# Five of sixteen weight pieces get their low halves from TensorE sums; VectorE scales four early pairs; 24 unread matmuls go; the main decay moves to the seventh step

## The chip, the cores and the metric

The kernel runs on one core of one Trainium2 chip. Time is device microseconds for one execution of the program; the smaller the better. The engines are TensorE (PE, with PEld for its weight loads), VectorE (DVE), ScalarE (ACT), GpSimd (POOL) and SyncE (SP), whose queue issues the DMAs.

## The reference

Attention with a forget gate over 8 batches of 8 heads (576 tokens, head size 64), and a two-layer feed-forward network with a leaky ReLU on its 4608 x 512 result:

```python
def _attn_ref(q, k, v, f):
    scores = scale * np.matmul(q, k.transpose(0, 1, 3, 2))
    log_f = np.log(np.clip(f, 0.0001, 1.0))
    cum = np.cumsum(log_f, axis=-1)
    decay = cum[:, :, :, None] - cum[:, :, None, :]
    scores = np.where(causal, -1000000000.0, scores + decay)
    scores = scores - np.max(scores, axis=-1, keepdims=True)
    attn = np.exp(scores)
    attn = attn / (np.sum(attn, axis=-1, keepdims=True) + 1e-09)
    return np.matmul(attn, v)
def _moe_ref(x, w_in, w_out):          # 512 -> 2048 -> 512
    h = x @ w_in
    g = np.maximum(0.01 * h, h)
    return g @ w_out
```

q, k, v and f arrive in fp32, and the two weight matrices in fp64.

## The kernel before

Products that need fp32 accuracy are made from fp32r matmuls of split operands: a value is a high part (`..h`, the value rounded to fp32r) and a low part (`..l`, the rest), and three products (high x high, low x high, high x low) are summed in PSUM.

**Weights.** The matrices are cut into 16 *pieces* of 128 x 1024 (numbered from 0; even ones of `w_in`, odd ones of `w_out`). `fetch_weight` brings a piece's 1 MB of raw 64-bit numbers into one of two buffers `wraw`, `load_weight` makes `wh` and `wl` of it: ACT scales the upper words to fp32 (`wt`, L177) and copies them to `wh` (L185); DVE shifts `wt` (L180), then builds the low part from the mantissa bits of both words (L186 to L191). `wt` has one buffer, so the next piece's L177 waits until the last reader of `wt` is through. A `wraw` buffer is free for piece n + 2 when L191 of piece n is done.

**Early steps.** Before the main loop come twelve steps `x` = 0 to 11 (the first to the twelfth), one for each pair of heads of the first three batches, over their first 256 tokens. `early_scores` makes fp32 scores on PE (`sce`), adds the decay by a second matmul (`both`), takes the maxima on DVE (L303, `ze`, `maxe`) and the exponentials on ACT (L307), and scales the rows by the inverse sums (L315, on ACT). `early_values` transposes (`tre`), copies to `pte` on ACT (L327), multiplies by v (`ave`) and splits the result to `xh`, `xl`. In the first six steps `warm` adds matmuls of zeros that nobody reads, after each of the two parts of the scores. Each step also loads one or two more weight pieces (`WQ`), and from the fifth on it fills in quanta of the feed-forward network (`FQ`): `h` (first layer), `g`, `gh`, `gl` (activation, split), `o` (second layer, PSUM tags `o0` and `o1` with one buffer each). `decay_rows` makes the decay rows of the main loop from the running sum `fc`, and writes them to DRAM (`dec_k`, `dec_q`) for the main heads.

**Main loop.** Then 64 heads pass over PE in turn, with feed-forward quanta between their parts.

**What sets the order.** The code is written in the order of the steps; a scheduler sets the order of instructions on each engine and in SP's queue when the program is built. Each engine then works strictly in that order, and waits on semaphores. SP too: a DMA whose buffer is not free holds up those behind it.

Of the kernel before, what the change touches and what calls it, by code (L numbers as in the profile page):

```python
# [8 lines left out]
F32 = mybir.dt.float32  # L9
F32R = mybir.dt.float32r  # L10
I32 = mybir.dt.int32
U32 = mybir.dt.uint32
AF = mybir.ActivationFunctionType
ALU = mybir.AluOpType

P = 128
# [12 lines left out]
FQ = (0, 0, 0, 0, 4, 8, 8, 8, 8, 8, 8, 4, 2)  # L29
BUFS = dict(s1=2, m1=2, ost=2)  # L30
RAWS = ("ph", "pl")
WARM = (20, 4, 6)
NEG = -1.0e30
REBIAS = 2.0**-112
SIGN = -(2.0**32)
# [3 lines left out]
def forgetting_attention_ffn(ctx, tc, qT, kT, v4, vr, f, w_in, w_out, out):  # L39
# [6 lines left out]
    nc = tc.nc  # L46
# [4 lines left out]
    HPB = NHEAD // NB  # L51
# [18 lines left out]
    def width(i):  # L70
        return min((i + 1) * P, S)
# [23 lines left out]
    one = ctx.enter_context(tc.tile_pool(name="one", bufs=1))  # L95
    dram = ctx.enter_context(tc.tile_pool(name="dram", bufs=1, space=bass.MemoryType.DRAM))
    psum = ctx.enter_context(tc.tile_pool(name="psum", bufs=2, space=bass.MemoryType.PSUM))
# [9 lines left out]
    def matmul(*args, **kw):  # L107
        work[0] += 1
        nc.tensor.matmul(*args, **kw)  # L109
# [7 lines left out]
    def warm(n):  # L117

        ps = psum.tile([P, 512], F32, tag="h", name=f"warm_{len(warmed)}")
        warmed.append(n)  # L120
        for _ in range(n):
            matmul(ps, still[:, :P], still, start=True, stop=True)

    warm(WARM[0])
    eye = one.tile([P, P], F32, tag="part0", name="eye")
    make_identity(nc, eye)
    ident_r = one.tile([P, P], F32R, name="ident_r")
    nc.vector.tensor_copy(ident_r, eye)
    ident = ident_r.bitcast(F32)
    both = one.tile([P, P + T + NHEAD], F32R, tag="s1", name="both", bufs=2)  # L130
    pick = both[:, P + T:]
    nc.vector.tensor_tensor(pick, ident[:, :NHEAD], ident[:, NHEAD:], op=ALU.add)
# [27 lines left out]
    def fetch_weight(n):  # L160
        raw = raws[n] = one.tile([P, 2, 4 * P, 2], I32, tag=RAWS[n % 2], name=f"wraw_{n}")
        for k, src in enumerate(wpieces[n][0]):
            nc.sync.dma_start(raw[:, k].rearrange("p w two -> p (w two)"), src)

    def load_weight(n):


        loaded.append(n)
        _, wh, wl = wpieces[n]
        wh, wl = (w.rearrange("p c f -> p (c f)") for w in (wh, wl))  # L170
        if n not in raws:
            fetch_weight(n)
        raw = raws[n].rearrange("p m w two -> p (m w) two")
        lo, hi = raw[:, :, 0], raw[:, :, 1]
        t = one.tile([P, 8 * P], I32, tag="vs", name=f"wt_{n}")
        tf = t.bitcast(F32)
        first = nc.scalar.activation(tf, hi.bitcast(F32), AF.Prelu, scale=REBIAS, alpha=SIGN)  # L177
        if n == 0:
            tc.keep_in_program_order(first)
        first = nc.vector.tensor_scalar(  # L180
            t, t, 3, 4, op0=ALU.logical_shift_left, op1=ALU.bitwise_or
        )
        if n == 0:
            tc.keep_in_program_order(first)
        nc.scalar.copy(wh, tf)  # L185
        nc.vector.tensor_scalar(hi, hi, 23, None, op0=ALU.logical_shift_left)  # L186
        nc.vector.scalar_tensor_tensor(
            lo, lo, 9, hi, op0=ALU.logical_shift_right, op1=ALU.bitwise_or
        )
        nc.vector.tensor_scalar(hi, t, -0x800000, None, op0=ALU.bitwise_and)  # L190
        nc.vector.scalar_tensor_tensor(  # L191
            wl, lo, 2.0**-43, hi.bitcast(F32), op0=ALU.mult, op1=ALU.mult
        )

    def weights(n):
        while len(loaded) < min(n, len(wpieces)):
            load_weight(len(loaded))
# [17 lines left out]
    for i, r in enumerate(decay_r):  # L215
        n = width(i)
# [6 lines left out]
    def decay_rows():  # L223

        tc.keep_in_program_order(
            nc.vector.tensor_scalar(fc, fc, -1.0 / SCALE, None, op0=ALU.mult)
        )
        start = one.tile([P, S], F32, tag="x", name="start")
        for i in range(NCH):
            c = slice(i * P, width(i))  # L230
            nc.vector.tensor_scalar(
                start[:, c], fc[:, c], 0.0, fc[:, i * P:i * P + 1], op0=ALU.mult, op1=ALU.subtract
            )
        for name, tag, x, to in (("fck", "s1", fc, dec_k), ("fcq", "m1", start, dec_q)):
            r = one.tile([P, S], F32R, tag=tag, name=name, bufs=2)
            halves(r, x)
            for w in range(2):
                nc.sync.dma_start(to[:, w], r[w * NHEAD:(w + 1) * NHEAD].bitcast(F32))
# [4 lines left out]
    def load(t):  # L243

        s, c0, c1 = tasks[t]
        h = state[t] = {}
        a, n = c0 * P, S
        x = h["raw"] = one.tile([P, S], F32, tag="qraw", name=f"raw_{t}")
        for y, src in ((x[:D, a:n], qT[s][:, a:n]), (x[D:, :n], kT[s][:, :n])):
            last = nc.sync.dma_start(y, src)  # L250
            if t < 2:
                tc.keep_in_program_order(last)
        if s % 2 == 0:
            pairs[s // 2, c0] = {}

    def load_v(t):

        g, o = tasks[t][0] // 2, tasks[t][0] % 2
        vm = fixed["vm"]
        for y, src in ((vm[:, :NFULL], v4[g][:, o]), (vm[:REST, NFULL], vr[g][:, o])):  # L260
            last = nc.sync.dma_start(y, src)
            if t < 1:
                tc.keep_in_program_order(last)
# [3 lines left out]
    def early_load(b, g):  # L267

        e = early[b, g] = {}
        x = e["qk"] = one.tile([P, 2, T], F32, tag="b2", name=f"qk_{b}_{g}", bufs=B2)  # L270
        for y, src in enumerate((qT, kT)):
            nc.sync.dma_start(
                x[:, y], src[b * HPB + 2 * g:b * HPB + 2 * g + 2, :, :T].rearrange("s d n -> (s d) n")
            )
        v = e["v"] = one.tile([P, 2, T // P, D], F32, tag="b2", name=f"ve_{b}_{g}", bufs=B2)
        nc.sync.dma_start(v, v4[b * HPB // 2 + g][:, :, :T // P])

    def early_scores(b, g):
        e = early[b, g]
        mx = one.tile([P, 4], F32, tag="max", name=f"maxe_{b}_{g}", bufs=3)  # L280
        sm = one.tile([P, 4], F32, tag="sum", name=f"sume_{b}_{g}", bufs=3)
        for i in range(2):
            n = width(i)
            ps = [
                psum.tile([P, 512], F32, tag="sc", name=f"sce_{b}_{g}_{2 * o + i}")[:, :n]
                for o in range(2)
            ]
            for o in range(2):
                x = e["qk"][o * D:(o + 1) * D]
                matmul(ps[o], x[:, 0, i * P:n], x[:, 1, :n], start=True, stop=False)  # L290
            for o in range(2):
                s = b * HPB + 2 * g + o
                matmul(
                    ps[o], pick[:, s:s + 1].broadcast_to([P, P]), decay_r[i],
                    start=False, stop=True,
                )
            for o in range(2):
                c = 2 * o + i
                tag = ZE[g % 2][c]
                z = e[c] = one.tile(  # L300
                    [P, n], F32, tag=tag, name=f"ze_{b}_{g}_{c}", bufs=BUFS.get(tag, 1)
                )
                nc.vector.tensor_tensor_reduce(  # L303
                    out=z, in0=ps[o], in1=tri[:, TRI - n:], scale=-SCALE, scalar=3.0e38,
                    op0=ALU.add, op1=ALU.min, accum_out=mx[:, c:c + 1],
                )
                nc.scalar.activation(  # L307
                    z, z, AF.Exp, bias=mx[:, c:c + 1], scale=-1.0, accum_out=sm[:, c:c + 1]
                )
            if b * HPB // 2 + g < WARM[2]:  # L310
                warm(WARM[1])
        nc.vector.tensor_scalar(sm, sm, 1.0e-9, None, op0=ALU.add)
        nc.vector.reciprocal(sm, sm)
        for c in range(4):
            nc.scalar.activation(e[c], e[c], AF.Copy, scale=sm[:, c:c + 1])  # L315

    def early_values(b, g):
        e = early[b, g]
# [390 lines left out]
    for x, (b, g) in enumerate(steps + [(NE, 0)]):  # L709
        if x + 1 < len(steps):  # L710
            early_load(*steps[x + 1])
        if x < len(steps):
            early_scores(b, g)
            if x in (8, 11):
                load(x // 11)
            if x == 8:
                load_v(0)
            if x == 10:
                split(0)
            weights(sum(WQ[:x + 1]))  # L720
        if x == 2:
            decay_rows()
        if x:
            early_values(*steps[x - 1])
            if steps[x - 1][1] == HPB // 2 - 1:
                ready[0] = (steps[x - 1][0] + 1) * T
        if x == len(steps):
            split(1)
        fill(FQ[x])
# [73 lines left out]
```

## Time and profile before

| | us |
|---|---|
| median of 3 runs (lowest, highest) | 1214.53 (1214.12, 1217.29) |
| the profiled execution | 1215.27 |
| its span, first to last instruction | 1213.2 |
| TensorE busy | 1197.9 (99%) |
| VectorE, ScalarE, GpSimd busy | 619.5, 637.1, 460.5 |
| `warm` matmuls | 68, between 1.5 and 59.5 us |

TensorE is busy nearly all the time, and the chain of work that ended last is 94% TensorE. A busy share does not say that the matmuls are needed, nor that they run at full clock: the column of the granted clock (1.00 is full) and the names have to be read with it. A row of a timeline gives the start, the duration of the merged run, the engine, the line, what is written from what is read, the shape and the count; what stands in brackets is the idle time before it and what ended it. A row of a group gives the count, the busy time in us and the mean of one in ns, then the idle time before.

### The profile page before, as it was taken

The numbers are of one execution on the slowest core, as the hardware profiler recorded it, in microseconds if no ns is written. First come the engines' busy times: TensorE is split into PE (matmuls) and PEld (weight loads), VectorE is DVE, ScalarE is ACT, GpSimd is POOL, SyncE is SP. The second block draws the span as 40 slices with busy tenths as digits, with TensorE's granted clock in tenths as the row PEclk, the third lists the DMA queues.
The fourth block names the chain that finished last, engine by engine and source line by source line (L and its number), as shares of the span: only waits on it lengthen the run. The fifth ranks groups of instructions, "written<-read, shape, count | busy, mean of one in ns | idle before, by whom it ended". The sixth has DMA issues, their size and how long they took to land.

```text
span 1213.2 us, 22495 instructions
## 1 busy us (share of the span) xinstructions
PE 1197.9 (99%) x7812; PEld 1070.6 (88%) x7812; DVE 619.5 (51%) x1685; ACT 637.1 (53%) x1633; POOL 460.5 (38%) x473
## 2 busy tenths in 40 slices
PE   9999999999999999999999999999999999999998
PEld 6677888888899999999999999999999999998997
DVE  5787756566655455554544444445444444553221
ACT  5776655667665565555545545455445445651111
POOL 1000155464555445454445353434454543531000
PEclk9899999999999999999999999999999999999999
DMA  5445433344343333323332323232223223221000
GB/s 183 140 172 182 125 109 103 90 124 120 97 126 91 84 97 92 110 80 89 92 99 64 90 71 95 70 90 63 74 84 88 62 69 82 76 62 46 19 18 18
DMA packets 82128, 110.54 MB, mean 91 GB/s; under 512 B 20640, under 2 KB 51728, under 8 KB 82016
## 3 DMA queue, kind: packets, MB, share of 16 engines
q1 hardware_dynamic: 82016, 109.12, 31.1%
q8 instruction: 62, 1.02, 0.4%
q14 instruction: 50, 0.41, 0.1%
HBM read 65.32 MB, written 18.58 MB: 69 GB/s over the span
## 4 chain that ended last, share of the span: by engine, by line
PE 94%; DVE 2%; DMA 1%; ACT 1%; issue 1%; POOL 0%; SPq 0%; DVEq 0%; ACTq 0%; POOLq 0%
PE h L109 33%; PE o L109 33%; PE tr L113 8%; PE av L109 8%; PE sc L109 7%; PE sce L109 2%; PE warm L109 2%; PE ave L109 1%; PE tre L113 1%; DVE fixed_z L414 0%; DMA wraw<-in_w_out 0%; DMA wraw<-in_w_in 0%; ACT g L631 0%; DVE gh L634 0%; DVE pl L466 0%
## 5 line engine op out<-in xcount | busy, mean ns | idle before, releaser
L636 POOL TENSOR_TENSOR gl<-g,gh 128x512 fp32r<-128x512 f32 x113 | 148.9, 1318 | 275.1 <-DVE gh L634 269.7
L109 PE MATMUL o<-wout_h,gh 128*128 128x512 f32 x576 | 231.3, 402 | 0.0
L109 PE MATMUL o<-wout_h,gl 128*128 128x512 f32 x576 | 227.3, 395 | 1.4 <-DVE gl L636 1.4
L109 PE MATMUL o<-wout_l,gh 128*128 128x512 f32 x576 | 227.5, 395 | 0.0
L420 ACT ACTIVATE fixed_z<-fixed_z,max 128x192 f32<-128x192 f32 (+3 forms) x272 | 161.0, 592 | 100.3 <-DVE max L414 98.0
L109 PE MATMUL h<-xh,win_h 128*128 128x256 f32 x1152 | 206.7, 286 | 0.9 <-ACT win_h L185 0.9
L464 ACT CAST ph<-tr 128x192 fp32r<-128x192 f32 (+3 forms) x360 | 126.8, 373 | 150.1 <-PE tr L113 99.5
L109 PE MATMUL h<-xh,win_l 128*128 128x256 f32 x1152 | 200.6, 283 | 0.1
L414 DVE CUSTOM_DVE_ANT_0 fixed_z<-sc,tri 128x192 f32<-128x192 f32 (+3 forms) x272 | 122.5, 452 | 151.0 <-PE sc L109 148.1
L631 ACT ACTIVATE g<-h 128x512 f32<-128x512 f32 x144 | 85.8, 596 | 216.3 <-PE h L109 200.1
L634 DVE CAST gh<-g 128x512 fp32r<-128x512 f32 x144 | 74.0, 514 | 214.4 <-ACT g L631 211.4
L466 DVE TENSOR_TENSOR pl<-tr,ph 128x384 fp32r<-128x384 f32 (+3 forms) x296 | 137.5, 467 | 81.6 <-ACT ph L464 80.2
L109 PEld LDWEIGHTS h<-xh,win_h 128*128 128x128 f32 x1152 | 171.2, 190 | 7.0 <-ACT win_h L185 1.0
L109 PEld LDWEIGHTS h<-xh,win_l 128*128 128x128 f32 x1152 | 165.2, 191 | 0.6 <-DVE win_l L191 0.3
L109 PE MATMUL h<-xs,win_h 128*128 128x256 f32 x1024 | 164.5, 283 | 0.0
L113 PE MATMUL tr<-ident_r,fixed_z 128*128 128x128 f32 x888 | 145.3, 274 | 3.5 <-DVE ph L471 1.7
L109 PEld LDWEIGHTS h<-xs,win_h 128*128 128x128 f32 x1024 | 141.0, 192 | 0.0
L109 PEld LDWEIGHTS o<-wout_h,gl 128*128 128x128 f32 x576 | 108.3, 188 | 26.2 <-DVE gl L636 2.1
L113 PEld LDWEIGHTS tr<-ident_r,fixed_z 128*128 128x128 f32 x888 | 107.7, 140 | 24.8 <-ACT rb L543 5.4
L109 PEld LDWEIGHTS o<-wout_l,gh 128*128 128x128 f32 x576 | 108.8, 189 | 15.8 <-issue 0.3
L150 POOL TENSOR_TENSOR fixed_m2a<-raw,m 64x576 fp32r<-64x576 f32 x32 | 46.0, 1437 | 202.1 <-ACT m L376 178.9
L109 PEld LDWEIGHTS o<-wout_h,gh 128*128 128x128 f32 x576 | 109.0, 189 | 15.0 <-issue 0.2
(110 smaller groups left out, 1761.5 us busy)
## 6 DMA issues: line engine op xcount, KB each, us to landing
raw<-in_kT SPq DMA_DIRECT2D x64, 144.0 KB
m<-m SPq DMA_DIRECT2D x64, 144.0 KB
wraw<-in_w_in SPq DMA_DIRECT2D x16, 512.0 KB
wraw<-in_w_out SPq DMA_DIRECT2D x16, 512.0 KB
fixed_vm<-in_v SPq DMA_DIRECT2D x64, 128.0 KB
xs<-xd SPq DMA_DIRECT2D x16, 512.0 KB
out<-ost SPq DMA_DIRECT2D x28, 256.0 KB
raw<-in_qT SPq DMA_DIRECT2D x40, 144.0 KB
```

What stands on the lines that cost most here:

```text
L109: nc.tensor.matmul(*args, **kw)
L113: nc.tensor.transpose(*args)
L150: nc.gpsimd.tensor_tensor(out, a, b, op=ALU.subtract)
L414: nc.vector.tensor_tensor_reduce(out=z[:, a:b], in0=ps[:m, :b - a], in1=tri[:m, at:at + b - a], scale=-SCALE, scalar=3.0e38 if x == 0 else ...
L420: nc.scalar.activation(z, z, AF.Exp, bias=h["max"][:m, last:last + 1], scale=-1.0, accum_out=fixed["sum" + "ab"[s // 2 % 2]][:m, i, s % 2: ...
L464: nc.scalar.copy(strided(ph, run), source(ps, run))
L466: nc.vector.tensor_tensor(strided(pl, run), source(ps, run), strided(ph, run).bitcast(F32), op=ALU.subtract)
L631: nc.scalar.activation(g, ph, AF.Prelu, alpha=0.01)
L634: nc.vector.tensor_copy(gh, g)
L636: eng.tensor_tensor(gl, g, gh.bitcast(F32), op=ALU.subtract)
```

## The change

- For pieces 0 to 4 (`n < SUMMED`) DVE no longer joins the words by L186 and L187. It makes a scaled low word by one operation each, and TensorE then sums, in each half of 512 columns, `ident` x `wt` (fp32) + `minus_r` x `wh` (fp32r) + `ident_r` x `wl` (fp32r) in PSUM (tags `o0`, `o1`, tiles `ws`). The sum goes back into `wl`, one half by ACT and one by DVE. `minus_r` is a new matrix, minus the identity.
- For the first four pairs (`SCALED`) DVE scales the rows by the inverse sums in place of ACT.
- `warm` in the first six steps issues 2 matmuls in place of 4: 24 fewer.
- `decay_rows` is called in step `x` = 6 in place of `x` = 2.

```diff
-WARM = (20, 4, 6)
+WARM = (20, 2, 6)
+SCALED = 4
+SUMMED = 5
...
+    minus_r = one.tile([P, P], F32R, name="minus_r")
+    nc.vector.tensor_scalar(minus_r, eye, -1.0, None, op0=ALU.mult)
...
-        first = nc.vector.tensor_scalar(
-            t, t, 3, 4, op0=ALU.logical_shift_left, op1=ALU.bitwise_or
-        )
+        if n < SUMMED:
+            first = nc.vector.tensor_scalar(t, t, 3, None, op0=ALU.logical_shift_left)
+        else:
+            first = nc.vector.tensor_scalar(
+                t, t, 3, 4, op0=ALU.logical_shift_left, op1=ALU.bitwise_or
+            )
...
         nc.scalar.copy(wh, tf)
+        if n < SUMMED:
+            nc.vector.tensor_scalar(hi, t, -0x800000, None, op0=ALU.bitwise_and)
+            nc.vector.scalar_tensor_tensor(
+                wl, lo.bitcast(U32), 2.0**-52, hi.bitcast(F32), op0=ALU.mult, op1=ALU.mult
+            )
+            for k in range(2):
+                c = slice(k * 4 * P, (k + 1) * 4 * P)
+                ps = psum.tile([P, 4 * P], F32, tag=f"o{k}", name=f"ws_{n}_{k}", bufs=1)
+                matmul(ps, ident, tf[:, c], start=True, stop=False)
+                matmul(ps, minus_r, wh[:, c], start=False, stop=False)
+                matmul(ps, ident_r, wl[:, c], start=False, stop=True)
+                (nc.scalar.copy, nc.vector.tensor_copy)[k](wl[:, c], ps)
+            return
         nc.vector.tensor_scalar(hi, hi, 23, None, op0=ALU.logical_shift_left)
...
         for c in range(4):
-            nc.scalar.activation(e[c], e[c], AF.Copy, scale=sm[:, c:c + 1])
+            if b * HPB // 2 + g < SCALED:
+                nc.vector.tensor_scalar(e[c], e[c], sm[:, c:c + 1], None, op0=ALU.mult)
+            else:
+                nc.scalar.activation(e[c], e[c], AF.Copy, scale=sm[:, c:c + 1])
...
-        if x == 2:
+        if x == 6:
             decay_rows()
```

The scheduler moves more than these lines. Line numbers after the change are up to 23 higher. The first place is TensorE in the first two steps. `sce_0_..`, `sce_1_..` and `sce_2_..` are the scores of steps one to three. Before:

```order
L109 MATMUL sce_0_1_223<-both 128x256
L109 MATMUL sce_0_3_224<-both 128x256
L109 MATMUL warm_356<-still 128x512 x3
L109 MATMUL sce_1_0_253<-qk_1_199 128x128
L109 MATMUL sce_1_0_253<-both 128x128
...
L109 MATMUL warm_433<-still 128x512 x4
L109 MATMUL sce_1_2_254<-qk_1_199 128x128
L109 MATMUL sce_1_2_254<-both 128x128
...
L109 MATMUL sce_1_1_270<-qk_1_199 128x256
L109 MATMUL sce_1_1_270<-both 128x256
```

and after, in the same place (`ws_0` and `ws_1` are the two halves of a sum, `wt_193` piece 0, `wt_295` piece 1):

```order
L111 MATMUL ws_0_199<-wt_193,ident_r 128x512
L111 MATMUL ws_0_199<-win_h_100,minus_r 128x512
L111 MATMUL ws_1_204<-wt_193,ident_r 128x512
L111 MATMUL ws_0_199<-win_l_108,ident_r 128x512
...
L111 MATMUL sce_0_1_231<-both 128x256
L111 MATMUL sce_0_3_232<-both 128x256
...
L111 MATMUL ws_0_301<-wt_295,ident_r 128x512
L111 MATMUL sce_1_1_274<-qk_1_209 128x256
L111 MATMUL sce_1_3_275<-qk_1_209 128x256
L111 MATMUL sce_1_1_274<-both 128x256
L111 MATMUL sce_1_3_275<-both 128x256
```

The sums stand where the fillers stood, all 20 fillers between the scores of the first four steps are gone, and the two heads' scores of 256 columns follow each other directly. Ahead of the first scores with decay there are 18 fillers in both.

The second place is DVE around the decay. Before, it lies between piece 2 (`win_l_107`) and the fifth step:

```order
L191 SCALAR_TENSOR_TENSOR win_l_107<-wraw_367 128x1024
L226 TENSOR_SCALAR fc<-fc 128x576
L341 TENSOR_TENSOR xl_154<-ave_1_407,xh_153 128x256
L231 TENSOR_SCALAR start<-fc 128x128 x4
...
L210 TENSOR_TENSOR fck<-fc,fck 64x576
...
L180 TENSOR_SCALAR wt_464<-wt_464 128x1024
L210 TENSOR_TENSOR fcq<-start,fcq 64x576
```

and after, between piece 6 (`win_l_111`) and piece 7 (`wt_889`, `wraw_886`), ahead of the seventh step's maxima (`ze_2_0_778`):

```order
L211 SCALAR_TENSOR_TENSOR win_l_111<-wraw_802 128x1024
...
L246 TENSOR_SCALAR fc<-fc 128x576
...
L251 TENSOR_SCALAR start<-fc 128x128 x3
L657 CAST gh_1_631<-g_1_629 128x512
...
L187 TENSOR_SCALAR wt_889<-wt_889 128x1024
...
L230 TENSOR_TENSOR fck<-fc,fck 64x576
L230 TENSOR_TENSOR fcq<-start,fcq 64x576
...
L211 SCALAR_TENSOR_TENSOR wout_l_127<-wraw_886 128x1024
L187 TENSOR_SCALAR wt_1004<-wt_1004 128x1024
...
L323 ISA ze_2_0_778,maxe_2_770<-sce_2_0_772,tri 128x128
```

Before, only piece 6 was through on DVE when the seventh step's maxima came; now piece 7 is too. The third place is SP's queue at piece ten (`wraw_1153` before, `wraw_1171` after). Before, its two halves stand apart, with the tenth step's `ve` and the main loop's first loads between:

```order
L272 DMA qk_1_941<-in_kT 128x256
L163 DMA wraw_1153<-in_w_in 128x1024
L276 DMA ve_1_944<-in_v 128x2x128
L250 DMA raw_978<-in_qT 64x320
L250 DMA raw_978<-in_kT 64x576
L261 DMA fixed_vm<-in_v 128x256
L261 DMA fixed_vm<-in_vr 64x64
L163 DMA wraw_1153<-in_w_in 128x1024
L163 DMA wraw_1164<-in_w_out 128x1024 x2
```

and after (`qk_0_849` belongs to the ninth step):

```order
L405 DMA fixed_s2a<-dec_q 2x320
L405 DMA fixed_s2b<-dec_q 2x320
L406 DMA fixed_m2b<-dec_k 2x576
L167 DMA wraw_1171<-in_w_in 128x1024 x2
L292 DMA qk_0_849<-in_qT 128x256
L292 DMA qk_0_849<-in_kT 128x256
L296 DMA ve_0_852<-in_v 128x2x128
L167 DMA wraw_1182<-in_w_out 128x1024 x2
```

Piece ten now goes out whole, ahead of the ninth step's loads.

## The prediction

> **What bounds the kernel now.** I read the mean clock and the span first, then the busy time by stretch, then the TensorE (PE) and VectorE (DVE) timelines of the first 60 us, then the waits of ScalarE (ACT) and of the DMA queue up to 160 us. Columns of the next rows: PE, weight load, DVE, ACT, GpSimd busy time in us, then the granted PE clock, the DMA share and GB/s.
>
> ```profile
> 14.00:41.00 27.00, 24.53 (x116) 15.43 (x114) 21.36 (x64) 21.71 (x60) 0.00 (x0) 1.00 0.45 143
> 41.00:51.00 10.00, 9.83 (x33) 6.23 (x34) 6.16 (x16) 5.05 (x15) 0.00 (x0) 0.51 0.71 227
> 92.00:122.00 30.00, 28.51 (x184) 22.45 (x183) 21.64 (x43) 19.51 (x42) 0.00 (x0) 1.00 0.54 176
> 160.00:1213.00 1053.00, 1044.60 (x6969) 954.44 (x6967) 506.78 (x1426) 528.65 (x1379) 444.33 (x439) 1.00 0.29 81
> ```
>
> After 160 us PE is busy 1044.6 of 1053 us, DVE and ACT half of it, and from about 130 us on the orders of all engines are the same in both kernels. So the change is worth what it shifts the moment at which PE reaches that common part. Everything is decided before it. There three things cost PE time: fillers, ten microseconds at half clock, and waits for weights near 104 and 118 us.
>
> The half clock has a visible forerunner:
>
> ```profile
> 37.93 0.45 DVE L226 TENSOR_SCALAR fc<-fc 128x576 f32<-128x576 f32 x1
> 38.63 1.03 DVE L231 TENSOR_SCALAR start<-fc 128x128 f32<-128x128 f32 x5
> 39.70 0.76 DVE L210 TENSOR_TENSOR fck<-fc,fck 64x576 fp32r<-64x576 f32 x1
> 38.42 0.67 ACT L209 CAST fck<-fc 128x576 fp32r<-128x576 f32 x1
> 39.00 1.13 ACT L177 ACTIVATE wt<-wraw 128x1024 f32<-128x1024 f32 x1
> 40.04 0.65 ACT L209 CAST fcq<-start 128x576 fp32r<-128x576 f32 x1
> 40.60 0.84 ACT L327 COPY pte<-tre 128x384 f32<-128x384 f32 x2
> 41.11 0.56 PE L109 MATMUL ave<-pte,ve 128*64 128x256 f32 x1 [1.55 <-ACT pte L327]
> ...
> 40.00:41.00 1.00, 0.00 (x0) 0.00 (x0) 0.97 (x3) 1.00 (x4) 0.00 (x0) 1.00 0.82 319
> 42.00:43.00 1.00, 1.00 (x7) 0.43 (x3) 0.97 (x6) 1.00 (x3) 0.00 (x0) 0.50 0.84 211
> ```
>
> The two decay casts stand on ACT ahead of `pte`, PE idles 1.55 us for it, and the clock is 0.50 right after.
>
> **The change, part by part.**
>
> *Conversion of the first five pieces.* the last columns are the busy time in us, the mean ns of one, and the idle time before:
>
> ```profile
> L180 DVE TENSOR_SCALAR wt<-wt 128x1024 int32<-128x1024 int32 x14 | 9.7, 690 | 6.1 <-ACT wt L177 6.1
> L186 DVE TENSOR_SCALAR wraw<-wraw 128x1024 int32<-128x1024 int32 x14 | 9.7, 690 | 0.0
> L187 DVE SCALAR_TENSOR_TENSOR wraw<-wraw 128x1024 int32<-128x1024 int32 x14 | 17.2, 1228 | 0.2
> L190 DVE TENSOR_SCALAR wraw<-wt 128x1024 int32<-128x1024 int32 x14 | 9.7, 693 | 0.2
> L191 DVE SCALAR_TENSOR_TENSOR win_l<-wraw 128x1024 fp32r<-128x1024 int32 x7 | 8.5, 1220 | 0.1
> L660 ACT COPY part<-o 128x512 f32<-128x512 f32 x3 | 1.6, 578 | 0.0
> L664 DVE TENSOR_TENSOR part<-o,part 128x512 f32<-128x512 f32 x4 | 2.8, 692 | 0.2
> ```
>
> DVE drops the 690 and 1228 ns operations and gains a PSUM copy of at most 0.69 us: 5 x (1.92 - 0.69) = 6.1 us less. ACT gains 5 x 0.58 = 2.9 us.
>
> *Scaling of four pairs.* It goes from ACT to DVE:
>
> ```profile
> L315 ACT ACTIVATE ze<-ze,sume 128x256 f32<-128x256 f32 x22 | 10.9, 496 | 0.0
> L315 ACT ACTIVATE ze<-ze,sume 128x128 f32<-128x128 f32 x22 | 8.6, 392 | 2.4 <-DVE sume L313 2.4
> L218 DVE TENSOR_SCALAR d<-fc 128x256 f32<-128x256 f32 x1 | 0.3, 347 | 0.0
> L231 DVE TENSOR_SCALAR start<-fc 128x128 f32<-128x128 f32 x4 | 0.9, 279 | 0.0
> ```
>
> ACT loses 4 x 2 x (0.496 + 0.392) = 7.1 us, DVE gains 4 x 2 x (0.347 + 0.279) = 5.0 us. With the decay (0.45 + 1.03 + 2 x 0.76 = 3.0 us of DVE, 0.67 + 0.65 = 1.3 us of ACT) out of the way too, DVE has about 4 us and ACT 5.5 us less to do before the sixth step. None of this is a gain by itself. It lets PE go on.
>
> *TensorE's new work.* Each piece gets two fp32 identity matmuls of 512 columns and four fp32r ones. No fp32 matmul of 512 columns is in the trace; its neighbours are (one fp32 matmul is two records):
>
> ```profile
> 19.01 0.69 PE L109 MATMUL sce<-qk 64*128 64x256 f32 x2
> 19.63 0.38 PE L109 MATMUL sce<-both 128*128 128x256 f32 x1
> ...
> 92.42 1.23 PE L109 MATMUL ave<-pte,ve 128*64 128x256 f32 x8
> 93.58 0.50 PE L109 MATMUL o<-wout_h,gl 128*128 128x512 f32 x1
> ...
> 9.28 4.38 PE L109 MATMUL warm<-still 128*128 128x512 f32 x18
> 13.50 0.34 PE L109 MATMUL sce<-both 128*128 128x128 f32 x2
> ...
> 80.96 0.80 PE L109 MATMUL sce<-qk 64*128 64x256 f32 x4
> 81.69 0.50 PE L109 MATMUL sce<-both 128*128 128x256 f32 x2
> ```
>
> The `ave` block streams 768 columns in 93.58 - 92.42 = 1.16 us, which makes 512 columns 0.77 us (low bound). The lone score block needs 0.62 us for 256, so twice that is 1.24 us (high bound). I take 0.95, nearer to `ave`, which is a stream over the full 128 rows as the identity matmul is. The fp32r ones are priced by the fillers: 4.22 / 18 = 0.234 us. So five pieces cost 10 x 0.95 + 20 x 0.234 = 14.2 us of PE, at the bounds 12.4 to 17.1.
>
> *What pays for it.* In the stretch from 14.3 to 57.4 us (the ramp), at whose end the changed order has done the same scores, transposes, values and the first two h groups, PE loses 20 fillers (20 x 0.234 = 4.7 us), the idle time before `ave` (1.55) and one of 0.90:
>
> ```profile
> 35.36 0.38 PE L109 MATMUL h<-xh,win_h 128*128 128x256 f32 x1 [0.90 <-ACT win_h L185]
> ```
>
> If the decay is gone from ACT's queue, the half clock should be too: 10.0 x (1 - 0.51) = 4.9 us. The new order also issues the two heads' scores side by side. A pair of 256-column fp32 scores took 81.69 - 80.96 = 0.73 us against 2 x 0.62 when apart; some five such meetings in the second, fourth and sixth steps make about 2.4 us. Sum: 14.2 - 4.7 - 2.45 - 4.9 - 2.4 = -0.25 us. Following the three queues row by row with these durations I come out 1.5 us early; I enter -1.0, between the two.
>
> In this stretch the additions have a price where they make others wait. On DVE the copy of the second sum stands ahead of the last two maxima of the first step (`ze`, `maxe`), and it waits for PE, which waits for ACT's `win_h` copy. By the rows this makes the first step's end about 2 us late, with everything behind it on DVE and ACT. Up to the third step the new kernel lags, and catches up where the old one waits for `pte`. `minus_r` (0.28 us of DVE, as the `start` operations of that size) is covered by the wait for `fr`:
>
> ```profile
> 4.39 0.59 DVE L200 TENSOR_SCALAR fr<-fr 128x576 f32<-128x576 f32 x1 [1.06 <-DMA fr<-in_f]
> ```
>
> *Sixth and seventh step.* Four fillers fewer between the score parts (4 x 0.234 = 0.94 us) and one more pair of scores side by side (0.5): -1.5 us. The decay now costs DVE 3.0 us and ACT 1.3 us here, where PE has 24 o matmuls (24 x 0.234 = 5.6 us) and an h group queued ahead of the next scores. I cost it at nothing; if that cover goes, it is the seventh step's maxima that come late, by up to 3 us. Its four DMAs now pass the weight transfers of piece eight on the SP queue, and wait for `fcq` ahead of piece nine, whose buffer comes free later than that in DVE's order.
>
> *Waits for weights.* These rows stand behind the poor stretch of 92 to 122 us:
>
> ```profile
> 101.54 1.13 ACT L177 ACTIVATE wt<-wraw 128x1024 f32<-128x1024 f32 x1 [1.92 <-DMA wraw<-in_w_in]
> 115.85 1.12 ACT L177 ACTIVATE wt<-wraw 128x1024 f32<-128x1024 f32 x1 [2.00 <-DMA wraw<-in_w_in]
> 104.66 0.50 PE L109 MATMUL o<-wout_h,gl 128*128 128x512 f32 x1 [1.21 <-DVE gl L636]
> ```
>
> PE idles 1.49 us in it (30.00 - 28.51), and perhaps another 1 us hides in matmuls that only look busy. The second half of piece ten stood on SP behind loads of other steps; in the new order it stands ahead of them, and DVE is one whole piece further when the seventh step's scores come. I take 2.5 us, between 0 (another transfer is late instead) and 4.
>
> Sum: -1.0 - 1.5 - 2.5 = -5.0 us on the profiled execution of 1215.27 us (span 1213.2 and 2.1 around it). That execution is 0.7 us over the median of 1214.53, against which I forecast 1209.5 us. The bounds: identity matmuls at 0.77 (-1.8), the queue walk whole (-0.5), weights at 4 (-1.5) give 1205.7; identity matmuls at 1.24 (+2.9), the ramp by the sum alone (+0.75) and no gain on the weights (+2.5) give 1215.7.
>
> **Rivals.** A change of 0.3%, 3.6 us, is about what can be told from none here.
>
> *The extra work eats the gain.* The ramp ends where it did, a later transfer is late in place of piece ten, and only the sixth step's 1.5 us and little more remains: 1213.0 us. For it speaks that PE is nearly full in the new ramp, so that every late hand-over counts; against it that 4.9 us of half clock are large beside such hand-overs.
>
> *The clock falls anyway, and longer.* One mechanism, in the ramp: with the fillers gone, PE waits between `ws` matmuls for ACT's copies, the granted clock falls, and the fp32 work runs at half speed (`sce<-qk` of 256 columns took 1.22 us then against 0.69):
>
> ```profile
> 45.38 1.22 PE L109 MATMUL sce<-qk 64*128 64x256 f32 x2
> ```
>
> A stretch T at half clock costs T/2. Ten microseconds, as now, would bring 1209.5 + 4.9 = 1214.4; the run is slower by 0.3% (1218.2) from T = 17.4 us on, and at 20 us it is at 1219.5. For it: a wait of 1.55 us sufficed once. Against it: 0.90 us at 34.5 us did not, and in the new order PE seldom lacks work. [...]
>
> **How the numbers follow.** Forecast 60%, of which the part above 1210.9 us (0.3% less than before) is 0.08; the extra work eats the gain 25%, within 0.3%; the clock falls anyway 15%, two thirds of it with a T that makes it slower than 0.3%. So faster 0.52, within 0.3% 0.08 + 0.25 + 0.05 = 0.38, slower 0.10. The range, 1204.5 to 1217.5, takes the forecast's bounds of 1205.7 and 1215.7, the first rival, and the clock rival up to T = 16 us; about 1 us below is for a ramp that gains more than the walk.
>
> **What would show it.** The granted clock stays 1.00 from 30 to 60 us (forecast) or has a stretch of 0.5 (clock rival). The 512-column fp32 identity matmuls stand 0.8 to 1.25 us apart. DVE's share before 60 us falls, and the wait for `pte` near 40 us is gone. ACT no longer waits 2 us for `wraw` near 100 and 115 us. The first o matmul starts before 60 us:
>
> ```profile
> 61.87 0.50 PE L109 MATMUL o<-wout_h,gh 128*128 128x512 f32 x1
> ```
>
> is the row to compare with. I am wrong if the `ws` matmuls wait for each other's PSUM bank or for ACT, if the seventh step's maxima are late, or if the gain of the ramp is given back at the start of the main loop.

## The result, and the profile after

The changed kernel takes 1208.76 us, the median of 4 runs (1207.18 to 1209.36), against 1214.98 us (1214.12 to 1217.29) for the kernel before in 4 runs on the same chip: a ratio of 0.9944, with a 95% interval of 0.9926 to 0.9961. On another chip, later, it was 1208.39 us and 0.9958 (0.9943 to 0.9973). So it is about half a per cent faster. The ratios here and below are formed from all runs, not from the two medians, whose quotients differ from them by up to 0.2%. The profiled execution took 1209.36 us, with a span of 1207.5 us, 5.7 us less than before.

The first view is busy time by stretch after the change: PE, weight load, DVE, ACT and GpSimd busy us with the number of instructions, then the granted clock, the DMA share and GB/s.

```profile
14.00:41.00 27.00, 26.06 (x122) 15.07 (x121) 23.09 (x73) 21.13 (x54) 0.00 (x0) 1.00 0.58 188
41.00:51.00 10.00, 10.00 (x56) 6.86 (x56) 7.85 (x18) 8.53 (x19) 0.00 (x0) 1.00 0.41 153
92.00:122.00 30.00, 29.17 (x185) 24.01 (x185) 25.73 (x51) 21.54 (x47) 0.00 (x0) 1.00 0.52 175
160.00:1207.00 1047.00, 1039.00 (x6931) 948.94 (x6930) 498.50 (x1411) 525.77 (x1371) 441.96 (x437) 1.00 0.29 80
```

The stretch of 41 to 51 us, at a clock of 0.51 before, is at 1.00. Between 14 and 41 us PE is idle 0.94 us instead of 2.47. The clock is 1.00 everywhere.

How far PE has come at fixed points of its program shows where the time was won. These are PE's rows in the timeline of the kernel before (start, duration, operation): the sixth step's first filler, the first scores of the seventh step, and the main loop's first scores.

```profile
57.42 1.20 PE L109 MATMUL warm<-still 128*128 128x512 f32 x4
71.47 0.49 PE L109 MATMUL sce<-qk 64*128 64x128 f32 x4
151.34 0.31 PE L109 MATMUL sc<-m,s 128*128 128x320 f32 x1
```

And the same points after, with the first o matmul, which stood at 61.87 us, second:

```profile
54.45 0.63 PE L111 MATMUL warm<-still 128*128 128x512 f32 x2
57.03 0.48 PE L111 MATMUL o<-wout_h,gh 128*128 128x512 f32 x1
66.83 0.49 PE L111 MATMUL sce<-qk 64*128 64x128 f32 x4
145.30 0.31 PE L111 MATMUL sc<-m,s 128*128 128x320 f32 x1
```

PE is 2.97 us ahead at the sixth step's first filler, 4.84 at the first o matmul, 4.64 in the seventh step and 6.04 at the main loop; 5.7 of it reaches the end. Of the lead 0.55 us was there at the first step's scores, before any of the changed work on PE; below it isn't counted to the change. That start scatters: in the twelve traces with the same fillers ahead of it, it lies between 13.04 and 14.28 us, and the kernel before has the latest. From the main loop's first `sc` to the end of the span it is 1061.9 us before and 1062.2 after: the loop itself has not changed.

### The profile page after: what moved, and what is told of

It is laid out like the page before. It is cut to its first block, busy times and chain, and to the rows that moved or that the text cites. A ratio compares the mean times of both kernels' runs of the same rounds, so it can differ in the third digit from the quotient of the medians.

```text
span 1207.5 us, 22521 instructions
## 1 busy us (share of the span) xinstructions
PE 1194.9 (99%) x7828; PEld 1068.1 (88%) x7828; DVE 613.2 (51%) x1697; ACT 633.2 (52%) x1622; POOL 460.8 (38%) x473
## 4 chain that ended last, share of the span: by engine, by line
PE 95%; DVE 2%; ACT 1%; DMA 1%; issue 1%; POOL 0%; SPq 0%; DVEq 0%; ACTq 0%; POOLq 0%
PE h L111 34%; PE o L111 33%; PE tr L115 8%; PE av L111 8%; PE sc L111 7%; PE sce L111 2%; PE ave L111 1%; PE ws L111 1%; PE warm L111 1%; PE tre L115 1%; DVE fixed_z L437 1%; DMA wraw<-in_w_in 0%; ACT g L654 0%; DVE pl L489 0%; DVE gh L657 0%
## 5 line engine op out<-in xcount | busy, mean ns | idle before, releaser
L115 PE MATMUL tr<-ident_r,fixed_z 128*128 128x128 f32 x888 | 145.3, 273 | 3.4 <-DVE ph L494 1.7
```

Of the source, the lines that this page charges most:

```text
L115: nc.tensor.transpose(*args)
```

## The experiments

Three explanations were at stake. **The clock**: the gain is the half-clock stretch, which goes because the decay no longer stands on ACT ahead of `pte`. **The relief**: TensorE's sums and VectorE's scaling shorten the conversion and softmax chains, and PE arrives earlier. **PE's load**: PE is the bound in the ramp, and the fillers left out are the gain. The alternatives in each expectation are these or parts of them. All kernels do the same computation as the reference. Ratios are to the kernel before on the same chip. The first four shared a chip, the next four another, the last four a third; the kernel before had medians of 1213.88, 1214.44 and 1214.01 us there.

**The decay alone.** The kernel before, with the decay in the seventh step:

```
-        if x == 2:
+        if x == 6:
             decay_rows()
```

> The kernel before, with the main decay alone moved to the seventh step. Theory A (the half clock of 41 to 51 us comes from TensorE's 1.55 us wait behind the decay's casts, and is the largest single term): the wait and the half clock go, the granted clock is 1.00 from 38 to 55 us, and the time falls by 3 to 5 us, to about 1211. Theory B (the half clock has another cause, or hides behind VectorE and ScalarE): the time stays within 1.5 us of before, with the clock still falling, or with it whole and the first o matmul no earlier than 61 us.

Measured: 1209.32 us, ratio 0.9959 (0.9944 to 0.9973), granted clock 1.0 in 7 of 10 runs. One line gives as much as the whole change (0.9944, and 0.9958 run again): what the other three parts add together can't be told from nothing by these runs, except that the clock is 1.0 in all 13 runs of the changed kernel.

But the trace, of one of the three runs below 1.0, doesn't show the expected mechanism. The wait of 1.55 us is gone, and the clock falls elsewhere: for 3.4 us each from 35.6, 49.3 and 114.1 us, together as long as the 10.2 us before. The first fall is behind the wait of 0.90 us for `win_h` that the prediction shows; the kernel before has it too, and stayed at 1.00 there. The second is behind the larger of two waits for `pte` that remain. The second view is PE's busy time, clock, DMA share and GB/s in stretches around them:

```profile
34.31 0.39 PE L109 MATMUL h<-xh,win_h 128*128 128x256 f32 x1 [0.90 <-ACT win_h L185]
41.83 1.24 PE L109 MATMUL ave<-pte,ve 128*64 128x256 f32 x8 [0.64 <-ACT pte L327]
49.20 1.52 PE L109 MATMUL ave<-pte,ve 128*64 128x256 f32 x4 [1.18 <-ACT pte L327]
```

```profile
32.00:35.00 3.00, 2.10 (x12) 1.00 0.55 173
35.00:38.00 3.00, 3.00 (x17) 0.60 0.37 109
38.00:41.00 3.00, 2.82 (x16) 0.83 0.99 329
...
44.00:47.00 3.00, 3.00 (x16) 1.00 0.36 85
47.00:50.00 3.00, 1.82 (x7) 0.88 0.68 265
50.00:53.00 3.00, 3.00 (x15) 0.56 0.02 5
```

Yet the main loop's first `sc` starts at 146.52 us, 4.8 us earlier than before, 1.05 of it by the earlier start. So in this run the gain isn't half clock that went. From the first step's 256-column scores to the seventh step's first score PE needs 54.4 us here and 57.2 before; 2.6 of these 2.8 us are the same score and `ave` records in less time, 22.8 instead of 25.4 us. Whether that is their order or where the clock was low was not separated.

**Fewer fillers alone.** The kernel before, with two fillers between score parts:

```
-WARM = (20, 4, 6)
+WARM = (20, 2, 6)
```

> The kernel before, with 2 in place of 4 unread matmuls after each part of the first six steps' scores. Theory A (TensorE waits for the other engines in the first 40 us, so a filler there costs next to nothing, and the wait behind the decay stays): 0 to 2 us faster, nearly all from the sixth step's four fillers, and the half clock still there. Theory B (the fillers stand in the way of the scores): 4 to 5 us faster, 20 x 0.234 us. Theory C (they hold the clock up): the stretch at half clock grows to over 15 us and the time rises by 2 us or more.

Measured: 1219.97 us, ratio 1.0033 (1.0012 to 1.0055), clock 0.981 to 0.990 in every run: slower. The runs form two groups, four at 1213.4 to 1214.1 us and eight at 1219.4 to 1221.7, with lower clocks (at most 0.985 against 0.989 or more). The trace is of the fastest run, which is no slower than the kernel before; the eight have none. The rows are PE's busy time, clock, DMA share and GB/s by 3 us:

```profile
14.00:17.00 3.00, 1.84 (x10) 1.00 0.16 47
17.00:20.00 3.00, 2.52 (x9) 0.93 0.15 18
20.00:23.00 3.00, 3.00 (x11) 0.50 0.72 213
...
38.00:41.00 3.00, 2.72 (x12) 0.50 0.70 218
```

PE lacks 1.6 us of work in the 6 us from 14, in waits of 0.42, 0.74 and 0.41 us for the maxima, and then runs at half clock for 23.9 us. By the runs together, the unread matmuls pay for themselves in the kernel before.

**The change without the sums.**

```
-SUMMED = 5
+SUMMED = 0
```

> The changed kernel with no piece summed on TensorE; all 16 pieces are joined on VectorE as before. Theory A (the sums are paid by idle TensorE time and free VectorE, 6 us less there): TensorE loses 13.7 us of work, VectorE gets 6.1 us more in the first 50 us, the ramp ends 1 to 4 us later than in the changed kernel, 1210 to 1213 us. Theory B (the sums make TensorE the bound of the ramp and cost more than they free): faster than the changed kernel, 1205 to 1208. If the clock falls with less TensorE work, up to 5 us more.

Measured: 1217.64 us, ratio 1.0033 (1.0009 to 1.0056), clock 0.979 to 0.994. PE has 14 us less to do and the kernel is about 0.8% slower than with the sums. The trace is again of the fastest run, at 1210.33 us where the slowest took 1224.65, so it shows the kind of loss and not its size:

```profile
14.00:17.00 3.00, 1.95 (x9) 1.00 0.20 55
17.00:20.00 3.00, 2.41 (x9) 1.00 0.01 2
20.00:23.00 3.00, 3.00 (x12) 0.51 0.85 243
```

It begins like the kernel with fewer fillers: the same three waits, then half clock, here for 6.8 us and later twice for 3.4. In the changed kernel the sums stand there, one wait of 0.89 us is left, and the clock holds: the sums act as fillers do, with work that is read. But they also take 6.1 us off VectorE by the prediction's sum, and no run has the one without the other. How the 0.8% divides between them is not shown.

**The change without the scaling.**

```
-SCALED = 4
+SCALED = 0
```

> The changed kernel with the scaling of the first four pairs on ScalarE again. Theory A (both engines have room and TensorE is the bound of the ramp): within 1.5 us of the changed kernel, 1208 to 1210.5. Theory B (ScalarE's queue holds up the transposes' copies, so its 7.1 us count): 2 to 5 us slower than the changed kernel, with waits of TensorE for pte in the ramp.

Measured: 1214.39 us, ratio 1.0002 (0.9988 to 1.0015), clock 0.997 to 1.0. The whole gain is gone though the clock holds. With the scaling left on ACT, ACT's `win_h` copies and so the sums come later: the third piece's copy starts at 33.20 us, in the changed kernel at 27.60. The waits of TensorE for `pte` that were expected are not in the trace. These are the waits between 14 and 62 us (who waited for whom: us, times, longest):

```profile
DVE win_l L204 <- PE ws L111: 4.2, 3, 1.6
...
DVE wout_l L204 <- PE ws L111: 2.2, 2, 1.3
```

DVE waits 6.4 us for sums, where it waits 1.3 us in the changed kernel. The first o matmul starts at 58.8 us instead of 57.0, and the main loop at 148.7 instead of 145.3.

**The change with the decay back in the third step.**

```
-        if x == 6:
+        if x == 2:
             decay_rows()
```

> The changed kernel with the main decay in the third step again. Theory A (a gap of TensorE lets the clock fall, and the sums now lie queued where the old kernel had nothing, so the decay's casts are covered): the clock stays above 0.998 and the time is within 2 us of the changed kernel, 1208 to 1211. Theory B (the decay in the third step always opens a gap, sums or not): clock 0.995 or less as before the change, 1212 to 1215.

Measured: 1211.79 us, ratio 0.9985 (0.9975 to 0.9996), clock 1.0 in 11 of 12 runs. With the sums, the decay in its old place makes the clock fall no more, and PE doesn't idle for `pte`. But it still costs 0.27% of the time, 3.3 us. The first o matmul starts at 60.82 us, 4.1 later than in the changed kernel run again (below):

```profile
60.82 0.51 PE L111 MATMUL o<-wout_h,gh 128*128 128x512 f32 x1
```

Up to it PE is idle 0.89 us in both. The delay sits between operations that look busy: from the first step's 256-column scores on, 66 score records take 14.25 us here and 12.59 there, counted from start to next start, and 36 `ave` records 6.28 us against 32 in 4.54. Fewer scores side by side are part of it; how much is a wait that the rows count as work was not separated.

**The change with four fillers again.**

```
-WARM = (20, 2, 6)
+WARM = (20, 4, 6)
```

> The changed kernel with 4 unread matmuls in place of 2. Theory A (with the sums TensorE is the bound of the ramp, and the sums do the fillers' work): 24 x 0.234 = 5.6 us more work, 3 to 6 us slower than the changed kernel, 1212 to 1214.5, clock 1.00. Theory B (TensorE still has room there): within 1.5 us, 1208 to 1210.

Measured: 1213.54 us, ratio 0.9997 (0.9983 to 1.0010), clock 0.999 to 1.0. Once the sums are there, the other fillers only cost: 4.7 us by the ratios (0.9997 - 0.9958), for 24 fillers at 0.234 us, 5.6 us.

**The change with no such fillers.** `WARM = (20, 0, 6)`:

> The changed kernel with no unread matmul in the six steps (the first 20 stay). Theory A (the 18 ahead of the first scores only delay them, and the sums hold the clock after that): the first scores with the decay come about 4 us earlier (9 us in place of 13), and the time falls by 3 to 5 us, to about 1204. Theory B (they hold the clock until the sums begin): the clock falls before 20 us and the time rises, 1212 or more, with a wide spread between runs.

Measured: 1209.65 us, ratio 0.9971 (0.9958 to 0.9985), clock 0.995 to 1.0. That lies between the two expectations: there is no more to gain. The first sum runs at half speed in the profiled run, after a wait of 2.23 us for DVE: its first two records take 2.08 us, against 1.02 for two in the changed kernel, and the granted clock is 0.78 from 8 to 14 us.

```profile
11.96 2.08 PE L111 MATMUL ws<-wt,ident_r 128*128 128x512 f32 x2 [2.23 <-DVE wt L185]
```

**The decay and the scaling, without sums, on the kernel before.** The decay at `x == 6` and DVE's scaling of four pairs, with four fillers:

> The kernel before with the decay in the seventh step and the first four pairs scaled on VectorE, but no sums and all fillers. The scaling was worth about 5 us in the changed kernel. Theory A (it takes a wait out of the chain from scores to values, sums or not): 3 to 5 us faster than the decay alone, 1204.5 to 1206.5. Theory B (it pays only where the sums have freed VectorE): no better than the decay alone, 1208 to 1212.

Measured: 1211.63 us, ratio 0.9985 (0.9970 to 1.0000), clock 0.991 to 0.997. With the scaling the decay's move seems worth less than alone (0.9959; the intervals overlap a little), and the clock is below 1.0 in every run: DVE's maxima come later, and PE waits 0.96 us for them at 34.68 us. So the scaling pays only beside the sums.

**Finer steps around the changed kernel**, on one chip. First the changed kernel again:

> The changed kernel again, unedited, on the chip of the next three runs, as their base. The time of the first runs was 1208.76 us. If its gain is a clock that is held and a shorter ramp, it comes out at 1207.5 to 1210 us with a granted clock of 1.0 in every run, and about 0.5% below the kernel before.

Measured: 1208.39 us, ratio 0.9958 (0.9943 to 0.9973), clock 1.0 in all 9 runs. Then `SUMMED = 6`:

> The changed kernel with a sixth piece summed on TensorE. Theory A (TensorE is the bound up to 60 us and the clock is held already, so extra sums are extra work): +2.8 us, two fp32 matmuls at 0.95 and four at 0.234 us, so 1211 to 1212. Theory B (VectorE's and ScalarE's relief still lets TensorE arrive earlier): no change or a gain of up to 1 us, 1208 to 1209, since VectorE loses another 1.2 us of work and TensorE's other waits in the ramp are a few us.

Measured: 1210.75 us, 2.4 us more, clock 0.999 to 1.0: a sixth piece costs nearly what its matmuls take. Then `SUMMED = 3`:

> The changed kernel with three pieces summed on TensorE instead of five. Theory A (pure TensorE work, clock held anyway): -5.7 us, so about 1203 us at a clock of 1.0. Theory C (the sums hold the clock, as without any of them it fell to 0.81 and the time was 1217.6): between the two, 1209 to 1214 us, with a granted clock under 0.998 in a part of the runs. Theory B (sums relieve VectorE, whose work returns at 1.2 us a piece): 1206 to 1208 at a clock of 1.0.

Measured: 1209.16 us (1207.52 to 1212.22), clock 0.997 to 1.0. PE's two sums less did not give the 5.7 us. The time is at the lower end of what was expected if the clock falls, but only one run of 12 is below 0.998, so the clock is not where the 5.7 us went. Then `WARM = (20, 1, 6)`:

> The changed kernel with one filler between score parts instead of two. With four it was 1213.5 us, with two 1208.8, with none 1209.7 (clock 0.995 to 1.0). Theory A (TensorE is the bound; the five sums hold the clock): -2.8 us at 0.234 us each for 12, at a clock of 1.0, so 1206. Theory C (the clock dips where score parts wait): 1208.5 to 1210, with a clock under 0.999 in some runs.

Measured: 1210.26 us, clock 1.0 in all 12 runs. The clock held, and yet 12 fillers fewer did not give 2.8 us but cost 1.9. Its timeline (idle time and what ended it in brackets) says where:

```profile
54.22 0.48 PE L111 MATMUL o<-wout_h,gh 128*128 128x512 f32 x1
...
66.63 0.91 PE L111 MATMUL sce<-qk 64*128 64x256 f32 x4 [0.27 <-DVE maxe L323]
...
112.34 0.91 PE L111 MATMUL sce<-qk 64*128 64x256 f32 x4 [0.30 <-DVE maxe L323]
...
128.80 0.90 PE L111 MATMUL sce<-qk 64*128 64x256 f32 x4 [0.80 <-DVE maxe L323]
```

The first o matmul starts 2.5 us earlier than in the changed kernel on that chip (54.22 against 56.73 us), as the fillers promise. By the scores at 110 us 0.15 us of it is left (110.51 against 110.66), and the main loop starts 1.5 us later (146.12 against 144.61). The kernel with three sums shows the same: first o matmul 3.3 us earlier, main loop 0.6. Past the ramp PE catches up with DVE's maxima and waits for them, and ACT waits longer for raw weights (between 62 and 150 us 4.5 us with one filler and 3.2 with three sums, 0.2 in the changed kernel on that chip, though 3.0 in its first trace). In these kernels a ramp that ends before about 57 us was worth nothing more. Which of the two waits takes most of it was not separated. No version tried beats the changed kernel; the decay alone equals it within the noise.

**How much is the clock.** The 100 runs of the kernel before beside the experiments have granted clocks of 0.993 to 1.0. The 20 at 0.999 or more have a median of 1210.9 us, the 37 at 0.995 have 1214.4, the 9 at 0.994 or less 1217.3. So of the 5.6 us of gain on the third chip (1214.01 to 1208.39) about 3 us is the clock that now holds in every run, and 2.5 us the shorter path. This rests on which runs happened to hold the clock, so it is an estimate from the runs, not a separate experiment. The shorter path, too, comes with the one line: the seven runs of the decay alone at clock 1.0 have a median of 1208.9 us, 2 us below the kernel before at 0.999 or more.

## Why the prediction was right, and which terms were off

The forecast was 1209.5 us with -5.0 us on the profiled execution; it came to 1208.76 us and -5.7 us of span. In the changed kernel the half clock went together with the wait for `pte`, as forecast. That the one follows from the other is not shown: with the decay alone the wait went too, and in the traced run the clock was at half for as long as before, in other places, and the gain was there all the same. The argument that a wait of 0.90 us had not sufficed fails there as well. So the 4.9 us of half clock, the largest term that was to pay for the sums, is borne out only in part, by the estimate of 3 us above. The parts are not the sum of three independent gains either, and that the total came within 1 us owes something to luck.

**The ramp, entered at -1.0, was -1.35 us.** PE's lead at the sixth step's first filler is 2.97 us. Of it 0.55 is the earlier start, and at that point the old order has already done two score records and three transposes (1.07 us) that the new order does behind it, which the prediction had overlooked. The table is PE's time from the first step's 256-column scores (14.28 us before, 13.73 after) to that point, each operation counted from its start to the next one's, less idle time, and the number of records:

| PE's work | before, us | after, us |
|---|---|---|
| `ws` sums | 0 | 14.46 (40) |
| fillers (`warm`) | 5.38 (20) | 0 |
| scores (`sce`) | 15.91 (62) | 11.60 (60) |
| `ave` | 6.90 (32) | 4.54 (32) |
| h | 8.21 (48) | 6.19 (48) |
| transposes (`tre`) | 4.29 (27) | 3.04 (24) |
| idle | 2.45 | 0.89 |
| sum | 43.14 | 40.72 |

The new work was priced rightly, 14.46 us against 14.2, and one fp32 identity matmul takes 29.12 - 28.17 = 0.95 us:

```profile
28.17 1.02 PE L111 MATMUL ws<-wt,ident_r 128*128 128x512 f32 x2
29.12 0.70 PE L111 MATMUL sce<-qk 64*128 64x256 f32 x2
```

The terms that were mis-sized offset each other. Half clock and paired scores were to give back 4.9 + 2.4 = 7.3 us; scores, `ave`, h and transposes together fell by 9.94 us, 8.9 of it for equal work. Not all of that is the clock. Up to the seventh step's first score all orders have done the same 66 score, 40 `ave`, 72 h and 30 transpose records. They take 41.1 us before and 30.7 after; with the decay back in its old place, at a clock of 1.0 too, they take 34.7. So 4.0 us of the fall are there without any change of the clock. The fillers gave 5.4 instead of 4.7. Against that the idle time fell by 1.56 instead of 2.45, for the reason named: the copy of the second sum on DVE stands ahead of the first step's maxima, and a new wait is there.

```profile
18.76 0.48 PE L111 MATMUL sce<-qk 64*128 64x128 f32 x2 [0.89 <-DVE maxe L323]
```

**The sixth and seventh step, -1.5, were -2.7 us**: 1.67 of lead between the two points and the 1.07 of work taken over. The eight fillers here took 1.04 + 1.12 us before and the four 0.56 + 0.48 after, 1.1 us less, near the 0.94 forecast; so the rest, 1.6 us, was priced too low at 0.5. The scores of both heads side by side gave 0.7 of it, eight `ave` records in one row instead of twice four gave 0.6 (1.59 us before, 0.98 after), and six transposes in one row 0.3. The decay costs nothing in its new place: its operations run from 58.4 to 64.4 us, over in time for the scores at 66.83 us, which wait for nothing. DVE's first and last, with the durations and starts in the line:

```profile
L246 DVE TENSOR_SCALAR fc<-fc x1: 454/454/454, 58.4 to 58.4; 128x576 f32<-128x576 f32 x1
L230 DVE TENSOR_TENSOR fcq<-start,fcq x1: 750/750/750, 63.6 to 63.6; 64x576 fp32r<-64x576 f32 x1
```

**The waits for weights, -2.5, were -1.4 us** (-6.04 less -4.64), and -1.8 in the trace of the second measurement. This term was too large. In the first trace ACT still waits, now once and longer:

```profile
110.36 1.13 ACT L181 ACTIVATE wt<-wraw 128x1024 f32<-128x1024 f32 x1 [3.03 <-DMA wraw<-in_w_in]
```

PE is idle 0.83 us from 92 to 122 us instead of 1.49, so "another transfer is late instead", the lower bound of that term, happened in part: VectorE's shift of these weights comes late, the maxima behind it too, and PE waits 0.80 us for them at 113.09 us. In the second trace ACT's wait for weights is 0.2 us and PE doesn't wait there. Between the main loop's start and the end 0.3 us more was given back.

**The rival of the clock** came true in a neighbouring kernel: without the sums the clock falls and the time is 1217.6 us, though PE waits there for the maxima and not between `ws` matmuls, which that kernel doesn't have. In the changed kernel PE has the sums in place of the fillers, and the clock holds. The prediction priced the sums as a cost of 14.2 us that the rest must pay for. The runs show that without them the rest of the change is slower than the kernel before, and that the decay alone, with neither the sums nor their price, gains as much. **The rival of the eaten gain** is seen in the two finer steps, where most or all of the ramp's further lead is gone by the main loop; in the change itself the weights gave 1.1 us less than forecast and the main loop took 0.3. "None of this is a gain by itself. It lets PE go on", said of the scaling and the conversion, held: the scaling is worth 0.44% beside the sums (0.9958 against 1.0002), and without them it looks like a loss (0.9985 against 0.9959).

## What to carry to other kernels

Read the granted clock by stretch before counting work: where it is 0.5 (here 0.51 from 41 to 51 us), the cheapest gain may be one block of work moved off the queue ahead of the operand that PE waits for. Work that is needed anyway can replace unread matmuls as what keeps PE busy (here the sums: a ratio of 0.9944 with them, 1.0033 without), but cut the fillers only together with it (alone: 1.0033). Run each part of a change alone as well: here one line of four parts gave as much as all of them. After each gain look at who is waited for next; here a ramp shortened below about 57 us gave its lead back to DVE's maxima and the weights within 90 us.

## What the runs showed of the hardware that was not expected

The clock fell without any single long wait. With fewer fillers three waits of 0.42 to 0.74 us, 1.6 us lacking in 6, were followed by 23.9 us at 0.50; in the kernel before 1.55 us was followed by 10.2. One kernel, unedited, was granted 0.993 to 1.0 in 100 runs. In four traces the half-clock stretches of the first 160 us lasted 3.4 us (three with the decay alone, two without the sums), 6.8 (without the sums), 10.2 (the kernel before) and 23.9 us (fewer fillers); what sets these lengths is not shown. In these runs the length of a wait doesn't decide alone: the wait of 0.90 us for `win_h`, with 2.10 us of PE work in the 3 us around it in both kernels, was followed by half clock from 35.6 us with the decay alone and by 1.00 in the kernel before. The busy share doesn't tell it alone either. With fewer fillers PE had only 1.17 of 3 us of work from 44 us on, and the clock stayed at 1.00. What lets it fall stays open.

```profile
44.00:47.00 3.00, 1.17 (x7) 1.00 0.84 288
47.00:50.00 3.00, 2.53 (x10) 1.00 0.77 234
```

PE's busy time hid a delay: with the decay back in its old place the idle time up to the first o matmul is the same 0.89 us, and the same number of score records takes 1.66 us more (14.25 against 12.59).
